# Window attention feeding a two-layer network: output copies ahead of a global softmax, early scores for a step's second head, and keys split two heads ahead

## The chip, the cores and the metric

The kernel runs on one core of one Trainium2 chip. Its time is the device time of one execution in microseconds (us), and the time of a kernel is the median over several runs. The engines are named as the profile names them: PE (TensorE matmul) with PEld (its weight load), DVE (VectorE), ACT (ScalarE), POOL (GpSimd), and SP, whose queue (SPq) issues the DMA transfers.

## What is computed

Eight sequences have eight heads each, with 512 local and 32 global positions and a head dimension of 64. The reference, cut to what matters:

```python
k_all = np.concatenate([k_g, k_l], axis=2)
v_all = np.concatenate([v_g, v_l], axis=2)
out_g = np.matmul(sm(scale * np.matmul(q_g, k_all.transpose(0, 1, 3, 2))), v_all)
s_ll = scale * np.matmul(q_l, k_l.transpose(0, 1, 3, 2))
mask = np.abs(pos[:, None] - pos[None, :]) <= 32
s_ll = np.where(mask, s_ll, -1000000000.0)
s_lg = scale * np.matmul(q_l, k_g.transpose(0, 1, 3, 2))
out_l = np.matmul(sm(np.concatenate([s_lg, s_ll], axis=-1)), v_all)
x = np.concatenate([out_g, out_l], axis=2)   # rows are tokens after a transpose
r = np.maximum(x @ w_in, 0.0)
out = (s * (r * r) + b) @ w_out
```

The local positions attend to a window and to the global positions. The global positions attend to everything. The 4608 tokens then pass through a network with 512 inputs, 2048 hidden values and 512 outputs.

## The kernel before

A "head" j in the code is one head of one half of a sequence (256 local tokens), so there are 128 of them. A token tile is 256 tokens, the 512 inputs of which are the outputs of eight heads. There are 16 such tiles and a 17th for the global tokens.

The kernel has two parts. The first 16 heads and the first eight steps of the network are written out by hand in a table (`PLAN`). Neither is touched by the change. The second part is a loop over `m`, called step m here, from 8 to 136. Step m does the attention work of one head, or of two in steps 12 and 14 (`TWO_HEADS`), then the first layer for two chunks of hidden values (`ffn_in(m)`), the activation (`relu`, `square`, `g_high`, `g_low`), and the second layer of the step before (`ffn_out(m - 1)`). Step 8 has head 16, step 12 heads 20 and 21, step 14 heads 23 and 24, and from step 15 on step m has head m + 10. A step's first head is `a`, its second is `z` (in the new code).

The work of one head j is:

- `split(j)`: ACT casts keys and queries to a short form (`kq`, two casts, L235 and L237), and POOL subtracts to get the rest (two subtractions, L236 and L238). It needs the loaded `rk` and `rq`.
- `products(j)`: PE computes the local scores into `ps_s` and the global ones into `ps_g`. Each has one buffer, so head j + 1 waits until both were read.
- `sm_scores` (DVE, L250, mask and row minimum, frees `ps_s`), `g_copy` (ACT, `tg`, L430) and `g_add` (DVE, L436, frees `ps_g`), `sm_exp` (ACT, L261), `sm_sums` and `sm_divide` (DVE, L268 to L277).
- `planes(j)`: DVE splits the result into 16-bit planes (`two`, one buffer, L453), and `turn(j)` sends them through a transposing DMA on SP's queue (`turned`, L459). `join(j)` on ACT puts them together one head later (`ptp`, two buffers for two pairs of heads, L467).
- `pv` on PE for four heads at a time (`ps_op`), whose result ACT copies into `x` (L392). For the global rows of half a sequence's heads there are `g_softmax` (DVE maximum L475, ACT exponential L481, DVE division L485 to L487), transposes, `g_pv` on PE, a copy `og` on ACT (L529), and a DMA to `xg_d` (L531).

After the last step of a token tile, `ffn_out` also copies the two accumulators out on ACT (`o`, L633). These tiles share the two buffers of tag `r` with the activations. This happens in the border steps 8, 16, 24 and so on.

On PE, ACT and DVE the order of the instructions is the order in which the code is written (`fixed.enter_context(tc.manual_schedule(...))`). The order on POOL and SP in the loop is made by a scheduler. Every queue is worked off in its order.

Of the kernel before, what the change touches and what calls it, by code (L numbers as in the profile page):

```python
# [11 lines left out]
F32 = mybir.dt.float32  # L12
# [4 lines left out]
I16 = mybir.dt.int16  # L17
# [3 lines left out]
B, H, SL, SG, D = 8, 8, 512, 32, 64  # L21
DM, DF = 512, 2048
P = 128
# [16 lines left out]
SGW = SL + SG  # L40
# [5 lines left out]
NF = 16  # L46
# [21 lines left out]
Q2 Fo6 Fr7 YA0 YA1 YB0 YB1 Fs7 Fb7 Fl7 Q3  # L68
""".split()
G_AT = (12, 16)  # L70
G_TR = 3
G_LD = 2
G_PV = 5


def f32(ap):
# [4 lines left out]
def window_attention_then_ffn(ctx: ExitStack, tc: tile.TileContext, qd, qp, qg, kw, vw, vg, w_in, w_out, out):  # L81
    nc = tc.nc
# [158 lines left out]
    def sm_scores(heads, scores):  # L241
        hf = slot(heads[0])[1]
        nm = sb.tile([P, 4], F32, tag="nm", name=f"nm{heads[0]}")
        parts = []
        for j, p_s in zip(heads, scores):
            sm = st_["p", j] = sb.tile([P, NC], F32, tag="sm", name=f"sm{j}", bufs=4)
            for blk in range(2):
                n, c = len(parts), COLS[hf, blk]
                mask = masks[hf == 0 and blk == 0][:, 0:c.stop - c.start]
                nc.vector.tensor_tensor_reduce(  # L250
                    out=sm[:, c], in0=p_s[:, c], in1=mask,
                    op0=ALU.add, op1=ALU.min, scale=-scale, scalar=BIG, accum_out=nm[:, n:n + 1],
                )
                parts.append(sm[:, c])
        st_["parts", heads[0]] = parts, nm
# [171 lines left out]
    def g_copy(j):  # L427
        ng = 256 + 32 * slot(j)[1]
        tg = st_["tg", j] = sb.tile([P, 288], F32, tag="tg", name=f"tg{j}", bufs=1)
        nc.scalar.copy(out=tg[0:32, 0:ng], in_=st_["pg1", j][32:64, 0:ng])  # L430
# [4 lines left out]
        p_g, tg = st_.pop(("pg1", j)), st_.pop(("tg", j))  # L435
        nc.vector.tensor_add(out=sg_rows(j, 32)[:, hf * 256:hf * 256 + ng], in0=p_g[0:32, 0:ng], in1=tg[0:32, 0:ng])  # L436

    def scores(j):
        products(j)
        sm_scores([j], [st_.pop(("ps1", j))])  # L440
        g_copy(j)
        g_add(j)
        sm_exp(j)
        sm_sums(j)
        sm_divide(j, False)
        planes(j)
# [42 lines left out]
    def g_softmax(b, g):  # L489
        g_max(b, g)  # L490
        g_exp(b, g)
        g_divide(b, g)
# [18 lines left out]
    def g_transposes(b, g):  # L511
        for part in range(2):
            g_turn(b, g, part)
            g_part(b, g, part)
            yield

    def g_load(b, g):
        rv = st_["rvg", b, g] = sb.tile([P, 4, 5, D], F32, tag="vsg", name=f"rvg{b}_{g}", bufs=1)
        nc.sync.dma_start(rv.rearrange("p h c d -> p (h c d)"), vg[b, g])
# [162 lines left out]
    assert not chunk_parts  # L682

    NM = NT * 8
    early, gpv, turns = defaultdict(list), defaultdict(list), {}
    for b in range(B):
        for g in range(2):
            s0 = 16 * b + G_AT[g]
            early[s0].append(lambda b=b, g=g: g_softmax(b, g))
            turns[s0 + G_TR] = g_transposes(b, g)  # L690
            early[s0 + G_LD].append(lambda b=b, g=g: g_load(b, g))
            gpv[s0 + G_PV].append(lambda b=b, g=g: g_pv(b, g))

    def head_work(j):
        if j < NS and j % 4 == 2:
            for i in (j // 2 - 1, j // 2):
                v_load(i)
        if j < NS:
            b1 = j // 16 + 1
            if j % 16 == 14 and b1 < B:  # L700
                qg_load(b1)
            scores(j)
            if j % 16 == 15 and j + 1 < NS:
                qg_split(b1)

    def values(j):
        if NF <= j - 5 < NS and j % 4 == 1:
            pv((j - 5) // 2, 2)
            pv_out((j - 5) // 2)
        for fn in gpv.pop(j, []):  # L710
            fn()

    def join_before(j):
        if NF <= j - 1 < NS:
            join(j - 1)

    def ends(j):
        for fn in early.pop(j, []):
            fn()

    load(NF + 2)
    j = NF
    for m in range(8, NM + 1):
        heads = [j, j + 1] if m in TWO_HEADS else [j]
        j = heads[-1] + 1
        a = heads[0]
        if a + 1 < NS:
            split(a + 1)
        for i in heads:
            if i + 3 < NS:  # L730
                load(i + 3)
        head_work(a)
        for i in heads[1:]:
            split(i + 1)
        values(a)
        t = m // 8 + 1
        if m < NM:
            ffn_in(m)
            if m % 8 == 7 and t < 16:
                x_split(t)  # L740
            relu(m)
            join_before(a)
            for c in LATER.get(m, ()):
                chunk_high(c)
            square(m)
            for c in LATER.get(m, ()):
# [7 lines left out]
        ends(a)  # L754
        for i in heads[1:]:
            head_work(i)
            values(i)
            join_before(i)
            ends(i)
        turn_g = [turns.pop(i) for i in heads if i in turns]  # L760
        ffn_out(m - 1, turn_g[0] if turn_g else iter(()))
    assert all(k < NF for d in (early, gpv, turns) for k in d)
    fixed.close()


# [74 lines left out]
```

## Time and profile before

| | |
|---|---|
| median of 3 runs | 968.01 us (967.84 to 969.32) |
| the profiled execution's own time | 969.22 us |
| its span, first to last instruction | 967.4 us |
| busy in the span | PE 937.0, PEld 837.2, DVE 649.1, ACT 708.7, POOL 219.0 us |

Most of the table speaks of the span of one profiled execution. Some 1.8 us of the execution's time lie around the span. A share of busy time is a mean over all stages, and the stages of this kernel have different limits.

### The profile page before, as it was taken

The numbers are of one execution on the slowest core, as the hardware profiler recorded it, in microseconds if no ns is written. First come the engines' busy times: TensorE is split into PE (matmuls) and PEld (weight loads), VectorE is DVE, ScalarE is ACT, GpSimd is POOL, SyncE is SP. The second block draws the span as 40 slices with busy tenths as digits, with TensorE's granted clock in tenths as the row PEclk, the third lists the DMA queues.
The fourth block names the chain that finished last, engine by engine and source line by source line (L and its number), as shares of the span: only waits on it lengthen the run. The fifth ranks groups of instructions, "written<-read, shape, count | busy, mean of one in ns | idle before, by whom it ended". The sixth has DMA issues, their size and how long they took to land.

```text
span 967.4 us, 20021 instructions
## 1 busy us (share of the span) xinstructions
PE 937.0 (97%) x7328; PEld 837.2 (87%) x7328; DVE 649.1 (67%) x1988; ACT 708.7 (73%) x1514; POOL 219.0 (23%) x245
## 2 busy tenths in 40 slices
PE   7899898999999999999999999999999999999996
PEld 3658787999999999999999999999999999988995
DVE  6999877777667666676667766776667766742221
ACT  6899687788778877788778877887788877742321
POOL 1010232232232322223323232332323222200000
PEclk7999999999999999999999999999999999999999
DMA  9953454454544564454454554456544554321000
GB/s 332 368 183 102 111 134 106 117 119 122 129 106 111 140 133 97 113 132 124 108 117 105 139 133 103 113 126 147 103 106 97 135 134 111 71 53 34 22 1 22
DMA packets 177610, 115.09 MB, mean 119 GB/s; under 512 B 125800, under 2 KB 166760, under 8 KB 177512
## 3 DMA queue, kind: packets, MB, share of 16 engines
q1 hardware_dynamic: 177368, 113.60, 45.1%
q8 instruction: 58, 0.95, 0.4%
q14 instruction: 40, 0.33, 0.1%
q10 hardware_dynamic: 144, 0.21, 0.1%
HBM read 74.98 MB, written 9.44 MB: 87 GB/s over the span
## 4 chain that ended last, share of the span: by engine, by line
PE 83%; DVE 9%; DMA 3%; ACT 2%; issue 1%; SPq 0%; DVEq 0%; ACTq 0%
PE ps_h L586 36%; PE acc L625 34%; PE ps_op L380 5%; PE ps_s L418 4%; DMA wst<-in_w_out 2%; DVE wst L184 2%; DVE we L190 1%; PE ps_g L422 1%; DVE wl L207 1%; PE ps_og L527 1%; DMA turned<-two 1%; PE ps_tg L505 1%; DVE we L174 1%; DVE r L598 1%; DVE g L606 1%
## 5 line engine op out<-in xcount | busy, mean ns | idle before, releaser
L586 PE MATMUL ps_h<-xs,wh 128*128 128x256 f32 x1584 | 288.2, 282 | 3.5 <-DVE r L598 2.8
L236 POOL TENSOR_TENSOR kq<-rk,kq 64x416 fp32r<-64x416 f32 x112 | 127.9, 1142 | 595.9 <-ACT kq L235 569.9
L625 PE MATMUL acc<-wh,g 128*128 128x512 f32 x792 | 248.9, 395 | 1.6 <-ACT o L633 1.6
L586 PEld LDWEIGHTS ps_h<-xs,wh 128*128 128x128 f32 x1584 | 243.4, 189 | 6.8 <-DVE r L598 3.0
L586 PE MATMUL ps_h<-xs,wl 128*128 128x256 f32 x792 | 220.1, 281 | 0.8 <-DVE wl L207 0.8
L606 DVE SCALAR_TENSOR_TENSOR g<-r,sb_t,g 128x512 fp32r<-128x512 f32 x133 | 100.5, 755 | 108.5 <-ACT g L602 108.5
L625 PEld LDWEIGHTS acc<-wh,g 128*128 128x128 f32 x792 | 140.6, 188 | 26.8 <-ACT o L633 1.8
L594 ACT ACTIVATE r<-ps_h 128x512 f32<-128x512 f32 x136 | 81.2, 597 | 107.7 <-PE ps_h L586 102.1
L625 PE MATMUL acc<-wl,g 128*128 128x512 f32 x396 | 155.2, 392 | 0.0
L467 ACT COPY ptp<-turned 128x1024 int16<-128x1024 int16 x112 | 152.0, 1358 | 1.5 <-DMA turned<-two 1.5
L586 PEld LDWEIGHTS ps_h<-xs,wl 128*128 128x128 f32 x792 | 149.4, 189 | 1.0 <-DVE wl L207 1.0
L598 DVE SCALAR_TENSOR_TENSOR r<-ps_h,sb_t,r 128x512 f32<-128x512 f32 x136 | 101.7, 748 | 67.3 <-ACT r L594 65.5
L602 ACT ACTIVATE g<-r,sb_t 128x512 fp32r<-128x512 f32 (+1 forms) x136 | 98.2, 722 | 57.2 <-DVE r L598 57.1
L261 ACT ACTIVATE sm<-sm,nm 128x224 f32<-128x224 f32 (+1 forms) x256 | 117.5, 460 | 6.4 <-DVE nm L250 3.7
L586 PE MATMUL ps_h<-xs,w 128*128 128x256 f32 x816 | 103.3, 282 | 0.0
L453 DVE COPY two<-sm 128x256 int16<-128x256 int16 x448 | 101.3, 291 | 1.9 <-DMA turned<-two 1.8
L586 PEld LDWEIGHTS ps_h<-xs,w 128*128 128x128 f32 x816 | 98.7, 189 | 2.0 <-issue 0.2
L625 PE MATMUL acc<-w,g 128*128 128x512 f32 x408 | 99.4, 392 | 0.1
L625 PEld LDWEIGHTS acc<-wl,g 128*128 128x128 f32 x396 | 74.3, 188 | 16.8
L625 PEld LDWEIGHTS acc<-w,g 128*128 128x128 f32 x408 | 74.2, 188 | 14.9 <-DVE g L606 0.5
L238 POOL TENSOR_TENSOR kq<-rq,kq 128x256 fp32r<-128x256 f32 x112 | 83.6, 747 | 8.8
L418 PE MATMUL ps_s<-kq 128*128 128x192 f32 (+1 forms) x448 | 78.6, 265 | 3.1 <-DVE nm L250 2.3
(77 smaller groups left out, 1123.6 us busy)
## 6 DMA issues: line engine op xcount, KB each, us to landing
rvp<-in_vw SPq DMA_DIRECT2D x64, 256.0 KB, 3.3
rq<-in_qd SPq DMA_DIRECT2D x112, 128.0 KB, 2.2
rk<-in_kw SPq DMA_DIRECT2D x56, 208.0 KB, 2.4
rvg<-in_vg SPq DMA_DIRECT2D x16, 640.0 KB, 4.7
out<-o SPq DMA_DIRECT2D x34, 256.0 KB, 2.1
wst<-in_w_in SPq DMA_DIRECT2D x16, 512.0 KB, 6.1
wst<-in_w_out SPq DMA_DIRECT2D x16, 512.0 KB, 6.9
turned<-two SPq DMA_TRANSPOSE x112, 3.1
```

Source lines behind the costliest of these rows:

```text
L236: nc.gpsimd.tensor_sub(out=ks[p1:p1 + 64], in0=rk[p0:p0 + 64], in1=f32(ks[p0:p0 + 64]))
L238: nc.gpsimd.tensor_sub(out=qs[:, 1, :], in0=rq, in1=f32(qs[:, 0, :]))
L261: nc.scalar.activation(out=p, in_=p, func=AF.Exp, bias=nm[:, n:n + 1], scale=-1.0, accum_out=ss[:, n:n + 1],)
L418: nc.tensor.matmul(p_s[:, cols], lhsT=qs[:, a, blk * P:(blk + 1) * P], rhs=ks[:, cols], start=(a == 0), stop=(a == 1),)
L453: nc.vector.tensor_copy(out=two[:, 2 * blk + c], in_=sm[:, :, c0:c0 + P])
L467: nc.scalar.copy(out=pt.bitcast(I16).rearrange("p c (q h) -> p c h q", h=2), in_=st_.pop(("turned", j)))
L586: nc.tensor.matmul(p_h[:, k], lhsT=weight(f, a)[:, c * P:(c + 1) * P], rhs=xcur[t][:, c, :] if m < PLAIN else xs_[t][:, e, c, :], start=(n ...
L594: nc.scalar.activation(out=r, in_=st_["ph", m], func=AF.Relu)
L598: nc.vector.scalar_tensor_tensor(out=r, in0=st_.pop(("ph", m)), scalar=s_t, in1=r, op0=ALU.mult, op1=ALU.mult)
L602: nc.scalar.activation(out=as_used(m, g[:, int(m < PLAIN)]), in_=st_["r", m], func=AF.Identity, bias=b_t)
L606: nc.vector.scalar_tensor_tensor(out=g[:, 1], in0=st_.pop(("r", m)), scalar=b_t, in1=f32(g[:, 0]), op0=ALU.add, op1=ALU.subtract,)
L625: nc.tensor.matmul(oacc[t][i], lhsT=as_used(m, g[:, a, k, i * P:(i + 1) * P]), rhs=weight(f, e)[:, 512:1024], start=(pr == 0 and n == 0), ...
```

## The change

The loop is written anew. Work per head and per step is the same, and no instruction is added or taken away. Four things move.

1. `split` runs two heads ahead in place of one. Step 10 (`CATCH_UP`) has one more split to get there. From then on step m splits head a + 2.
2. In a step with two heads, the products and the score maximum of the second head (`begin(z)`) come right after `ffn_in(m)`, ahead of the planes and the transposing DMA of the first (`turned(a)`). The rest of the second head (`weigh(z)`) stays behind `g_low(m)`.
3. In such a step `pv`, its copy, `g_pv` and its copy (`values(z)`) come behind `ffn_out(m - 1)`. They stood ahead of it and ahead of `join`.
4. The global softmax of the second half of the heads of sequence 0 moves from step 8 to step 9, and in border steps what is listed as `early` comes behind `ffn_out` with its output copies.

The functions `g_planes`, `g_turn_dma` and `g_join` are new, but with `G_PE = 8` and eight sequences no step calls them.

```diff
-            early[s0].append(lambda b=b, g=g: g_softmax(b, g))
+            early[s0 + int((b, g) == (0, 1))].append(lambda b=b, g=g: g_softmax(b, g))
...
+        if cut < NS and cut <= a + 2:
+            split(cut)
+            cut += 1
+        if a < NS:
+            begin(a)
+            weigh(a)
+        if z > a:
+            split(cut)
+            cut += 1
+        elif m == CATCH_UP:
+            split(cut)
+            cut += 1
+        if z == a:
+            values(a)
+        if m < NM:
+            ffn_in(m)
+            if z > a:
+                begin(z)
+        if a < NS:
+            turned(a)
...
+        if not border:
+            at(early, a)
+        if z > a:
+            weigh(z)
+            turned(z)
+            join_before(z)
...
         ffn_out(m - 1, turn_g[0] if turn_g else iter(()))
+        if border:
+            at(early, a)
+        if z > a:
+            values(z)
```

On ACT, from the end of step 8 to step 10, this stood before (`sg4` is the global score tile of the moved softmax, `o0_0` and `o0_1` are the output copies):

```order
L602 ACTIVATE g8_1137<-r8_1130,sb_t_71 128x512
L481 ACTIVATE sg4_226,gs0_1_1143<-sg4_226,gm0_1_1140 128x544
L633 COPY o0_0_1160<-acc0_0_557 128x512
L633 COPY o0_1_1163<-acc0_1_558 128x512
L235 CAST kq18_1166<-rk18_1065 64x416
...
L602 ACTIVATE g9_1261<-r9_1252,sb_t_71 128x512
L235 CAST kq19_1278<-rk18_1065 64x416
```

Now the same stretch of ACT reads as follows, up to the activation of step 10:

```order
L659 COPY o0_0_1152<-acc0_0_557 128x512
L659 COPY o0_1_1155<-acc0_1_558 128x512
L235 CAST kq18_1162<-rk18_1065 64x416
...
L628 ACTIVATE g9_1253<-r9_1244,sb_t_71 128x512
L485 ACTIVATE sg4_226,gs0_1_1259<-sg4_226,gm0_1_1256 128x544
L235 CAST kq19_1284<-rk18_1065 64x416
...
L261 ACTIVATE sm18_1297,ss18_1303<-sm18_1297,nm18_1296 128x224
L235 CAST kq20_1310<-rk20_1158 64x416
L237 CAST kq20_1310<-rq20_1160 128x256
L620 ACTIVATE r10_1347<-ps_h10_1315 128x512
```

The softmax went behind the activation of step 9, and step 10 got the casts of a second head.

On ACT in step 12, from the global copy of head 21 on, this stood before:

```order
L430 COPY tg21_1543<-ps_g21_1533 32x256
L261 ACTIVATE sm21_1540,ss21_1546<-sm21_1540,nm21_1539 128x192
L261 ACTIVATE sm21_1540,ss21_1546<-sm21_1540,nm21_1539 128x224
L392 COPY x2_1577<-ps_op8_1560 128x512
L529 COPY og0_1_1600<-ps_og0_1_1579 128x64
L467 COPY ptp10_1603<-turned20_1493 128x4x2x128
L235 CAST kq23_1617<-rk22_1368 64x416
```

Now the two copies `x2` and `og0_1` stand behind the join of head 20, which waits for a transposing DMA:

```order
L261 ACTIVATE sm21_1531,ss21_1551<-sm21_1531,nm21_1530 128x224
L471 COPY ptp10_1565<-turned20_1539 128x4x2x128
L392 COPY x2_1596<-ps_op8_1579 128x512
L555 COPY og0_1_1619<-ps_og0_1_1598 128x64
L235 CAST kq24_1628<-rk24_1462 64x416
```

On SP's queue of the new kernel the transfers of the same step stand like this. The store to `xg_d` stands ahead of the transposing DMA of head 21, as it did before, but it needs the copy `og0_1`, which is what moved:

```order
L463 DMA_TRANSPOSE turned20_1539<-two20_1534 128x8x128
L314 DMA rvp10_1624<-in_vw 128x2x256
L314 DMA rvp11_1626<-in_vw 128x2x256
L545 DMA rvg1_0_2362<-in_vg 128x1280
L557 DMA xg_d_112<-og0_1_1619 4x32x64
L463 DMA_TRANSPOSE turned21_1563<-two21_1558 128x8x128
```

On DVE in step 12 the new kernel has the score maximum of head 21 between the division and the planes of head 20:

```order
L277 TENSOR_SCALAR sm20_1479<-sm20_1479,ss20_1486 128x224
L250 ISA sm21_1531,nm21_1530<-ps_s21_1523,mask1_87 128x192
L250 ISA nm21_1530 128x1
L250 ISA sm21_1531,nm21_1530<-ps_s21_1523,mask0_95 128x224
L250 ISA nm21_1530 128x1
L457 COPY two20_1534<-sm20_1479 128x256 x4
```

Before, the maximum of head 21 stood behind `g_low(12)` there.

## Rows read from the trace of the kernel before

**Rows 1.** The span and the mean granted clock of the core.

```profile
core 0: 967.4 us, clock 0.989
```

**Rows 2.** Stretch, length, busy PE, PEld, DVE, ACT, POOL (instructions), granted clock, DMA, GB/s.

```profile
105.00:157.00 52.00, 45.34 (x382) 39.69 (x381) 39.89 (x126) 40.80 (x89) 16.13 (x18) 1.00 0.55 132
157.00:900.00 743.00, 743.00 (x6015) 679.04 (x6015) 501.49 (x1667) 564.03 (x1207) 194.61 (x210) 1.00 0.46 112
```

**Rows 3.** Waits of PE, 98 to 165 us: total, times, longest.

```profile
PE ps_s L418 <- DVE nm L250: 2.3, 1, 2.3
PE acc L625 <- ACT o L633: 1.6, 1, 1.6
...
PE ps_op L380 <- ACT ptp L467: 0.6, 1, 0.6
PE ps_s L418 <- POOL kq L238: 0.4, 1, 0.4
```

**Rows 4.** The chain that ended last, from 109 us: start, length, what.

```profile
123.09 4.76 DMA turned<-two
...
136.57 4.58 DMA turned<-two
```

**Rows 5.** Timeline of ACT, then DVE, steps 8 and 9: start, length, instruction, idle before.

```profile
108.20 0.73 ACT L602 ACTIVATE g<-r,sb_t 128x512 fp32r<-128x512 f32 x1 [1.21 <-DVE r L598]
...
112.50 0.54 ACT L235 CAST kq<-rk 64x416 fp32r<-64x416 f32 x1
...
109.21 0.75 DVE L606 SCALAR_TENSOR_TENSOR g<-r,sb_t,g 128x512 fp32r<-128x512 f32 x1
...
112.08 0.50 DVE L487 TENSOR_SCALAR sg<-sg,gs 128x544 f32<-128x544 f32 x1
```

**Rows 6.** Timeline of DVE, then POOL, heads 19 and 20 (steps 11 and 12).

```profile
127.29 0.57 DVE L277 TENSOR_SCALAR sm<-sm,ss 128x192 f32<-128x192 f32 x2
127.95 0.90 DVE L453 COPY two<-sm 128x256 int16<-128x256 int16 x4
...
133.77 1.43 DVE L277 TENSOR_SCALAR sm<-sm,ss 128x192 f32<-128x192 f32 x2
135.12 1.42 DVE L453 COPY two<-sm 128x256 int16<-128x256 int16 x4
...
133.77 1.07 POOL L236 TENSOR_TENSOR kq<-rk,kq 64x416 fp32r<-64x416 f32 x1 [0.26 <-ACT kq L235]
134.92 0.86 POOL L238 TENSOR_TENSOR kq<-rq,kq 128x256 fp32r<-128x256 f32 x1
```

**Rows 7.** Timeline of ACT, then SP's queue, end of step 12.

```profile
140.09 0.58 ACT L392 COPY x<-ps_op 128x512 f32<-128x512 f32 x1
140.58 0.22 ACT L529 COPY og<-ps_og 128x64 f32<-128x64 f32 x1
141.17 1.37 ACT L467 COPY ptp<-turned 128x1024 int16<-128x1024 int16 x1 [0.37 <-DMA turned<-two]
...
140.82 0.56 SPq L531 DMA_DIRECT2D xg_d<-og  x1
...
142.17 1.24 SPq L459 DMA_TRANSPOSE turned<-two  x1
```

**Rows 8.** The transposing DMA (tile `turned`), 100 to 200 us.

```profile
DMA to landing us min/median/max: 3.0/3.1/4.8
```

**Rows 9.** Timeline of DVE, then PE, steps 14 and 15.

```profile
155.30 0.75 DVE L606 SCALAR_TENSOR_TENSOR g<-r,sb_t,g 128x512 fp32r<-128x512 f32 x1 [0.79 <-ACT g L602]
...
156.55 0.44 DVE L436 TENSOR_TENSOR sg<-ps_g,tg 32x288 f32<-32x288 f32 x1
...
157.17 0.30 PE L422 MATMUL ps_g<-kq,qgs 128*64 128x288 f32 x1
```

**Rows 10.** Busy time and granted clock in two short stretches, columns as in rows 2.

```profile
154.00:157.00 3.00, 0.71 (x5) 0.32 (x4) 2.20 (x7) 1.72 (x5) 0.00 (x0) 1.00 0.63 136
157.00:162.00 5.00, 5.00 (x47) 4.60 (x47) 3.94 (x17) 4.16 (x11) 1.79 (x2) 0.66 0.50 83
```

More of the change, by code (lines that the diff above doesn't have):

```diff
@@ L70 @@
 G_AT = (12, 16)
-G_TR = 3
-G_LD = 2
 G_PV = 5
+G_PE = 8
+CATCH_UP = 10
 def f32(ap):
@@ L436, in g_add, with begin, weigh @@
         nc.vector.tensor_add(out=sg_rows(j, 32)[:, hf * 256:hf * 256 + ng], in0=p_g[0:32, 0:ng], in1=tg[0:32, 0:ng])
-    def scores(j):
+    def begin(j):
         products(j)
         sm_scores([j], [st_.pop(("ps1", j))])
+    def weigh(j):
         g_copy(j)
@@ L445, in scores, with turned @@
         sm_divide(j, False)
+    def turned(j):
         planes(j)
@@ L515, in g_transposes, with g_planes, g_turn_dma, g_join @@
             yield
+    def g_planes(b, g, c0, c1):
+        if c0 == 0:
+            two = sb.tile([P, 20 * P], I16, tag="vsg", name=f"gtwo{b}_{g}", bufs=1)[:, 0:10 * P]
+            st_["gtwo", b, g] = two.rearrange("p (c h k) -> p c h k", c=5, h=2)
+        sg = st_["sg", b, g].bitcast(I16).rearrange("p (k h) -> p h k", h=2)
+        for c in range(c0, c1):
+            s0 = min(c * P, SGW - P)
+            nc.vector.tensor_copy(out=st_["gtwo", b, g][:, c], in_=sg[:, :, s0:s0 + P])
+    def g_turn_dma(b, g):
+        both = sb.tile([P, 2 * JOINED[0][1]], I16, tag="pg", name=f"pg{b}_{g}", bufs=1)
+        turned, pg = both[:, 0:10 * P].rearrange("p (c h q) -> p c h q", c=5, h=2), both[:, 10 * P:20 * P]
+        nc.sync.dma_start_transpose(
+            turned.rearrange("p c h q -> p (c h) q"), st_.pop(("gtwo", b, g)).rearrange("p c h k -> p (c h k)"),
+        )
+        st_["turned_g", b, g] = turned, pg
+    def g_join(b, g, c0, c1):
+        turned, pg = st_["turned_g", b, g]
+        nc.scalar.copy(out=pg.rearrange("p (c q h) -> p c h q", c=5, h=2)[:, c0:c1], in_=turned[:, c0:c1])
+        st_["pg", b, g] = pg.bitcast(F32).rearrange("p (c r) -> p c r", c=5)
     def g_load(b, g):
@@ L684, in window_attention_then_ffn @@
     NM = NT * 8
-    early, gpv, turns = defaultdict(list), defaultdict(list), {}
+    early, gpv, joins_at, planes_at, turns = defaultdict(list), defaultdict(list), defaultdict(list), defaultdict(list), {}
     for b in range(B):
@@ L688, in window_attention_then_ffn, with head_loads @@
             s0 = 16 * b + G_AT[g]
-            early[s0].append(lambda b=b, g=g: g_softmax(b, g))
-            turns[s0 + G_TR] = g_transposes(b, g)
-            early[s0 + G_LD].append(lambda b=b, g=g: g_load(b, g))
+            early[s0 + int((b, g) == (0, 1))].append(lambda b=b, g=g: g_softmax(b, g))
+            if b < G_PE:
+                turns[s0 + 3] = g_transposes(b, g)
+                early[s0 + 2].append(lambda b=b, g=g: g_load(b, g))
+            else:
+                planes_at[s0 + 1].append(lambda b=b, g=g: g_planes(b, g, 0, 3))
+                planes_at[s0 + 2].append(lambda b=b, g=g: (g_planes(b, g, 3, 5), g_turn_dma(b, g)))
+                joins_at[s0 + 3].append(lambda b=b, g=g: (g_join(b, g, 0, 2), g_load(b, g)))
+                joins_at[s0 + 4].append(lambda b=b, g=g: g_join(b, g, 2, 5))
             gpv[s0 + G_PV].append(lambda b=b, g=g: g_pv(b, g))
-    def head_work(j):
+    def head_loads(j):
         if j < NS and j % 4 == 2:
@@ L697, in head_work, with at @@
                 v_load(i)
[L698 to L704, printed above, removed]
+        if j < NS and j % 16 == 14 and j + 16 < NS + 2:
+            qg_load(j // 16 + 1)
+    def at(hooks, j):
+        for fn in hooks.pop(j, []):
+            fn()
     def values(j):
@@ L709, in values @@
             pv_out((j - 5) // 2)
-        for fn in gpv.pop(j, []):
-            fn()
+        at(gpv, j)
     def join_before(j):
@@ L715, in join_before @@
             join(j - 1)
-    def ends(j):
-        for fn in early.pop(j, []):
-            fn()
     load(NF + 2)
-    j = NF
+    j, cut = NF, NF + 1
     for m in range(8, NM + 1):
@@ L725, in window_attention_then_ffn @@
         j = heads[-1] + 1
-        a = heads[0]
-        if a + 1 < NS:
-            split(a + 1)
+        a, z = heads[0], heads[-1]
+        border = (m - 1) % 8 == 7
         for i in heads:
@@ L731, in window_attention_then_ffn @@
                 load(i + 3)
[L732 to L735, printed above, removed]
+        for i in heads:
+            head_loads(i)
+        if cut < NS and cut <= a + 2:
[18 more added lines that the diff above has]
+            turned(a)
+            if a % 16 == 15 and a + 1 < NS:
+                qg_split(a // 16 + 1)
         t = m // 8 + 1
         if m < NM:
-            ffn_in(m)
             if m % 8 == 7 and t < 16:
@@ L742, in window_attention_then_ffn @@
             join_before(a)
+            at(joins_at, a)
             for c in LATER.get(m, ()):
@@ L745, in window_attention_then_ffn @@
             square(m)
+            at(planes_at, a)
             for c in LATER.get(m, ()):
@@ L753, in window_attention_then_ffn @@
             join_before(a)
[L754 to L759, printed above, removed]
+            at(joins_at, a)
+            at(planes_at, a)
+        if not border:
[4 more added lines that the diff above has]
+            join_before(z)
+            at(joins_at, z)
+            at(planes_at, z)
+            at(early, z)
         turn_g = [turns.pop(i) for i in heads if i in turns]
         ffn_out(m - 1, turn_g[0] if turn_g else iter(()))
-    assert all(k < NF for d in (early, gpv, turns) for k in d)
+        if border:
+            at(early, a)
+        if z > a:
+            values(z)
+    assert all(k < NF for d in (early, gpv, turns, joins_at, planes_at) for k in d)
     fixed.close()
```

## The prediction

> **What bounds the kernel now.** I read the span first [rows 1], then busy time by stretch, then what PE waits for, then the chain that ended last, and last the timelines of the engines in the stretch where PE waits. The reader is to see that there are two regimes. From 157 to 900 us PE is busy for 743.00 of 743.00 us at a granted clock of 1.00 [rows 2]: no order of other work can give anything there, and another order takes something only if it makes an engine late by more than its slack, and DVE and ACT are busy for only 501 and 564 us of it. From 105 to 157 us PE is busy for 45.34 of 52 us [rows 2], so 6.7 us is all that PE idles in the steps 8 to 15 that the change rearranges. PE's waits name the objects: 2.3 us for the score maximum, 1.6 us for the output copies, 0.6 us for a join, 0.4 us for a split [rows 3]; the rest are waits of under 1 us. The chain that ended last shows what makes PE wait there: before 157 us it runs mostly over ACT, DVE and two transposing DMAs of 4.76 and 4.58 us [rows 4], not over PE. In these steps the limit is a relay of ACT, DVE and the transposes, in which PE waits now at one place and now at another. So the question is what the change does to the relay, and the end of the kernel moves by what PE's restart near 157 us moves by.
>
> **Splits two ahead.** From step 15 on, a split has a step's time or more in hand, and PE's only wait for one that I count is 0.4 us, in step 14 [rows 3]. So in the steady steps this is worth nothing. Its price is the extra split in step 10. Its casts lie under ACT's wait for DVE, but its two POOL subtractions now fall beside head 18's division and planes, as they do in step 12 for head 20 already. What that does is in the trace: for head 19, with POOL quiet, division and planes take 0.57 and 0.90 us, for head 20, beside POOL subtractions of 1.07 and 0.86 us, they take 1.43 and 1.42 us [rows 6]. This is 0.86 + 0.52 = 1.4 us on DVE, and `square(10)`, which all that follows hangs on, stands behind them. In steps 12 and 14 the slow place exists before and after. The bounds are 0 (the subtractions fall a little earlier or later) and 1.4 us. I take **+1.2**, near the upper end, since the step has the same form.
>
> The Trainium skill (SBUF — State Buffer, Who interferes with whom) has a rule that speaks against this change: VectorE's copies and tensor_scalar operations in their two-port mode and GpSimd's operations exclude each other from a shared pair of ports, and the loser stands still for the other's whole instruction. By that rule the price would be up to both subtractions, 1.07 + 0.86 = 1.9 us, and the whole sum below 0.7 us higher; the row's 1.4 us is less, so I keep the row.
>
> **The softmax one step later.** Before, ACT ends `g_high(8)` at 108.93, waits for DVE's maximum, does the exponential and the two output copies, and only at 112.50 comes to the next cast; DVE's `g_low(8)` starts at 109.21 and ends at 109.96 [rows 5]. Now the first copy can start near 109.0. The second takes the buffer that `g_low(8)` reads, so it starts at 109.96 and ends about 0.5 us later, half the 0.96 us that both take in the chain; the cast comes at about 110.5, 2.0 us earlier, and PE's 1.6 us wait for the copies is gone. But the softmax now stands whole between `g_low(9)` and the score maximum of head 18. In step 8 DVE has from 109.96 to 112.58 for it, the end of its division (112.08 + 0.50) [rows 5], 2.6 us, which now delays head 18 because DVE's maximum and ACT's exponentials of head 18 queue behind it. The net is 2.6 - 2.0 = **+0.6**. The bounds are -2.0 (all of the second is hidden) and +1.0. This is a stall that moves: PE has it next at `ffn_out(10)`, waiting for `g_low(10)`.
>
> **The second head's early scores, step 12.** The score maximum of head 21 goes ahead of the planes of head 20. Its length is what lies between `g_low` and `g_add` in step 14, from 156.05 to 156.55 [rows 9], 0.5 us. Planes 20, `turn(20)` and `square(12)` come that much later; but the planes then fall behind POOL's subtractions in place of beside them, which gives back up to 0.5 us (1.42 - 0.90) [rows 6]. I take **+0.2**, between 0 and 0.5.
>
> **The late values, step 12.** Before, the copies `x` and `og` (0.58 and 0.22 us) lie in ACT's wait for the transposing DMA, ahead of the join at 141.17, and the `xg_d` store goes out at 140.82 in time for the transposing DMA of head 21 at 142.17 [rows 7]. Now they come behind the join. From the landing of transpose 20, ACT has the join (1.2 us of its 1.37, since the next one overlaps), and 0.5 + 0.2 us of copies, and the store takes 0.56 us on SP: 2.5 us until `turn(21)` can be issued, where it was 1.0 us (141.17 to 142.17). This is +1.5 us on SP's queue, and +0.7 us on ACT's next cast and copy, which DVE's `g_add(22)` waits for. Behind the store are queued the transposes 21 and all later loads, and DVE's planes 22 wait for transpose 21 because `two` has one buffer. Some of it was slack: transpose 21 landed near 145.3 (142.17 and the median 3.1) [rows 7, 8]. I take **+1.1**. The bounds: +1.5, and if transpose 20, which took 4.6 us [rows 4], now lands after the 3.1 us median [rows 8] because the `rvp` loads moved behind it, 1.5 us less, that is -0.4.
>
> **Step 14.** The score maximum of head 24 again goes ahead of planes 23 (+0.2, as above), but `g_add(24)` then follows `g_low(14)` directly, without the 0.5 us between them and a little of waiting [rows 9], -0.6. So **-0.4**. PE no longer waits 2.3 us for `ps_s`. It waits for `ps_g`, which `g_add(24)` frees: the products of head 25 get through their first three matmuls and stop there.
>
> **The sum** is 1.2 + 0.6 + 0.2 + 1.1 - 0.4 = +2.7 us. PE's `ps_g` matmul moves from 157.17 [rows 9] to about 159.9, and from there PE is the limit as before. The profiled execution took 969.22 us, so this form would take 971.9; against the median of 968.01, which is 1.2 us lower, it is **970.7 us**, 0.28% more.
>
> **The clock.** Right after PE's 2.3 us idle before 157 us, in a stretch where it was busy for 0.71 of 3.00 us, the granted clock falls, and is 0.66 on average from 157 to 162 us [rows 10]: the lower of the two levels for about two thirds of it, which costs (1 - 0.66) x 5.0 = 1.7 us of PE's work. The shorter waits left the clock at 1.00 [rows 2]. In the new form PE's idle time ahead of `ps_g` is about as long, so I take the drop as kept, 0 us. If it vanished it would give 1.7 us, and a further one would take as much where PE is not waiting anyway.
>
> **The rivals.** *PE's waits are the loss themselves (faster).* If the relay had room, each removed wait would count: 1.6 + 2.3 + 0.6 + 0.4 = 4.9 us, and with the clock drop gone another 1.7, so 968.0 - 4.9 = 963.1, at the least 961.4. For it speaks that each of these waits is at a point that the change touches; against it that the chain runs over the others there. It decides if DVE is through with `g_add(24)` before 155.0, that is if the terms sum to less than -1.9 us. A part of it, one of the costs absent and the clock drop gone, gives 964 to 966. Chance 0.15. *The costs mostly miss (no difference).* Transpose 20 lands after 3.1 us (-1.5) and the extra subtractions fall half beside idle DVE (-0.6): 970.7 - 2.1 = 968.6. The rows give both ends of both, so chance 0.33. *The change does nothing in the steady steps* is part of all cases: there it only makes a split earlier that nobody waits for.
>
> **How the numbers follow.** My forecast, slower by over 0.2% (about what a measurement of this kernel can tell from no change, 1.9 us), has a chance of 0.52. With the rival of no difference at 0.33 and the faster one at 0.15, these are also the chances of the three verdicts. The lower end of the range takes the sum without POOL's term (-1.2), with the fast transpose (-1.5) and without the clock drop (-1.7): 966.3. The upper end takes the upper bounds (1.4, 1.0, 0.5, 1.5 and 0, in all 4.4): 972.4, rounded to 972.6 for a drop that comes partly on top. What lies below 966.3 is some 0.12, above 972.6 some 0.06. The forecast's own range is 969.9 to 972.6.
>
> **What would show it right or wrong.** The wait of PE for the output copies in step 9 is gone, and a new one of 1 us or more stands at `ffn_out(10)` or at the next products. Division or planes of head 18 take over 1 us each beside POOL. ACT's `x` and `og` copies come right behind a join that waited, and SP's transposing DMA of head 21 follows the `xg_d` store at once. The last wait of PE near 159 us is for `ps_g`, on `g_add`, of 2 us or more, with a clock drop behind it, and after that the busy share of PE is full. I am wrong in the relay if `g_add(24)` ends before 156 us, in the POOL term if head 18 shows 0.57 and 0.90 us, in the late values if transpose 21 is issued less than 1.5 us after transpose 20 landed, and in the frame if PE waits after 165 us.

## The result, and the profile after

The changed kernel takes **973.95 us** (median of 6 runs, 973.65 to 976.11) against 968.02 us (967.84 to 969.50) for the kernel before in the same comparison: ratio 1.0062, interval 1.0052 to 1.0072, that is +5.9 us where +2.7 us was forecast, and outside the range given. The profiled execution took 973.65 us, against 969.22 us. This is +4.4 us; the rest is that the profiled execution of before lay 1.2 us above its median and this one 0.3 us below.

The same views in the same order. The span and mean clock, as [rows 1], then windows of both regimes (columns as in [rows 2]), with the stretch in which the clock now falls last:

```profile
core 0: 971.9 us, clock 0.989
```

```profile
105.00:162.00 57.00, 47.42 (x385) 41.33 (x383) 40.01 (x128) 41.46 (x92) 18.13 (x20) 0.97 0.51 121
162.00:904.00 742.00, 741.15 (x6008) 677.30 (x6009) 502.62 (x1669) 563.35 (x1207) 192.47 (x208) 1.00 0.46 112
119.00:126.00 7.00, 6.08 (x24) 5.25 (x25) 5.38 (x15) 4.75 (x14) 2.33 (x3) 0.76 0.05 12
```

From 162 us on PE is busy for 741.15 of 742.00 us, nearly as full as before from 157 us. So the loss lies ahead of that, in the relay of steps 8 to 15. PE idles there for 9.6 of 57 us, where it was 6.7 of 52 us [rows 2]. What it waits for, from 100 to 175 us (total, times, longest), answers to [rows 3]:

```profile
PE ps_g L422 <- DVE sg L436: 3.8, 3, 2.7
PE ps_h L612 <- ACT wh L202: 3.4, 1, 3.4
PE ps_s L418 <- DVE nm L250: 1.8, 1, 1.8
PE ps_h L612 <- DVE wl L207: 0.8, 1, 0.8
PE ps_op L380 <- ACT ptp L471: 0.4, 1, 0.4
```

The 1.6 us for the output copies are gone, and a wait of 3.4 us for ACT's cast of the weights is new. That cast is not late by itself. ACT's timeline of steps 8 and 9 (start, length, instruction, idle before it and who ended it) shows what stands ahead of it, beside [rows 5]:

```profile
108.65 0.72 ACT L628 ACTIVATE g<-r,sb_t 128x512 fp32r<-128x512 f32 x1 [1.20 <-DVE r L624]
109.28 0.56 ACT L659 COPY o<-acc 128x512 f32<-128x512 f32 x1
110.50 0.59 ACT L659 COPY o<-acc 128x512 f32<-128x512 f32 x1 [0.66 <-DVE g L632]
110.98 0.54 ACT L235 CAST kq<-rk 64x416 fp32r<-64x416 f32 x1
...
116.40 0.60 ACT L620 ACTIVATE r<-ps_h 128x512 f32<-128x512 f32 x1 [3.03 <-DMA out<-o]
...
118.08 1.03 ACT L202 CAST wh<-we 128x1024 fp32r<-128x1024 f32 x1
```

The copies and the cast come where the prediction has them, the cast at 110.98 us. But then `relu(9)` waits **3.03 us for the output store**: its tile `r` gets a buffer that the store still reads, since `o` and `r` share two buffers. SP's queue of the changed kernel and the time from a store's issue to its landing (the view gives one landing for the two stores), then the same in the kernel before, with ACT's `relu(9)` there and the instruction ahead of it:

```profile
107.98 1.97 SPq L463 DMA_TRANSPOSE turned<-two  x1
110.06 0.51 SPq L545 DMA_DIRECT2D rvg<-in_vg  x1
110.63 0.89 SPq L663 DMA_DIRECT2D out<-o  x2
...
DMA to landing us min/median/max: 5.8/5.8/5.8
```

```profile
112.15 0.82 SPq L637 DMA_DIRECT2D out<-o  x2
...
DMA to landing us min/median/max: 2.7/2.7/2.7
...
114.68 0.21 ACT L529 COPY og<-ps_og 128x64 f32<-128x64 f32 x1
114.98 0.60 ACT L594 ACTIVATE r<-ps_h 128x512 f32<-128x512 f32 x1
```

The stores go out 1.5 us earlier than before, and `relu(9)` starts 1.4 us later: at 116.40 us with the landing, where it was 114.98 us, 0.13 us behind a landing at 112.15 + 2.7 = 114.85 us. (The whole profile starts 0.46 us later; counted from `g_low(8)` the stores go out 2.0 us earlier and `relu(9)` starts 1.0 us later.) The store held `relu(9)` in the kernel before, too, for a time too short for the list of waits: there it starts 0.30 us behind the start of `og`, the instruction ahead of it, and 0.11 us behind it in a kernel in which it waits for no store (e2, below). So what moves earlier ahead of `relu(9)` gains nothing behind it as long as the store lands no earlier. The reader can find this only by asking who has the buffer next.

The other places, one fence for each group: head 18 on DVE and POOL (as [rows 6]), the end of step 12 on ACT and SP's queue (as [rows 7]), step 14 on DVE and PE (as [rows 9]).

```profile
125.67 1.36 DVE L277 TENSOR_SCALAR sm<-sm,ss 128x192 f32<-128x192 f32 x2
126.94 1.44 DVE L457 COPY two<-sm 128x256 int16<-128x256 int16 x4
...
125.58 1.08 POOL L236 TENSOR_TENSOR kq<-rk,kq 64x416 fp32r<-64x416 f32 x1 [0.17 <-ACT kq L235]
126.74 0.89 POOL L238 TENSOR_TENSOR kq<-rq,kq 128x256 fp32r<-128x256 f32 x1
```

```profile
144.84 1.37 ACT L471 COPY ptp<-turned 128x1024 int16<-128x1024 int16 x1 [0.52 <-DMA turned<-two]
146.23 0.59 ACT L392 COPY x<-ps_op 128x512 f32<-128x512 f32 x1
146.72 0.22 ACT L555 COPY og<-ps_og 128x64 f32<-128x64 f32 x1
...
141.63 1.23 SPq L463 DMA_TRANSPOSE turned<-two  x1
...
146.96 0.56 SPq L557 DMA_DIRECT2D xg_d<-og  x1
147.61 1.24 SPq L463 DMA_TRANSPOSE turned<-two  x1
```

```profile
161.27 0.75 DVE L632 SCALAR_TENSOR_TENSOR g<-r,sb_t,g 128x512 fp32r<-128x512 f32 x1 [0.79 <-ACT g L628]
161.94 0.44 DVE L436 TENSOR_TENSOR sg<-ps_g,tg 32x288 f32<-32x288 f32 x1
...
162.44 0.35 PE L422 MATMUL ps_g<-kq,qgs 128*64 128x288 f32 x1 [2.73 <-DVE sg L436]
```

### The profile page after: what moved, and what is told of

Its sections match the earlier page's. It is cut to its first block, busy times and chain, and to the rows that moved or that the text cites. A ratio compares the mean times of both kernels' runs of the same rounds, so it can differ in the third digit from the quotient of the medians.

```text
span 971.9 us, 20030 instructions
## 1 busy us (share of the span) xinstructions
PE 936.7 (96%) x7328; PEld 836.9 (86%) x7328; DVE 649.8 (67%) x1988; ACT 708.4 (73%) x1514; POOL 218.4 (22%) x245
## 4 chain that ended last, share of the span: by engine, by line
PE 83%; DVE 9%; DMA 3%; ACT 2%; issue 2%; SPq 0%; DVEq 0%; ACTq 0%
PE ps_h L612 36%; PE acc L651 35%; PE ps_op L380 5%; PE ps_s L418 4%; DVE wst L184 2%; DMA wst<-in_w_out 1%; PE ps_g L422 1%; DVE wl L207 1%; DVE we L190 1%; PE ps_og L553 1%; PE ps_tg L509 1%; DVE r L624 1%; DVE we L174 1%; DMA turned<-two 1%; DVE sm L250 1%
```

## The experiments

Twelve kernels ran, each timed in 5 rounds beside the kernel before. Runs of one kernel spread over 1.7 to 6 us here, so the table gives the ratio to the kernel before with its interval, and that ratio times 968.02 us. The next columns are starts of DVE instructions in the profiled execution, counted from `g_low(8)`, ahead of which nothing differs (109.21 us before, 109.67 us after, 108.2 to 110.4 us in the others). "Wait" is that of `relu(9)` for the store as the view lists it; in e1 `relu(9)` is idle for 0.34 us, which the view puts down to PE, and a wait for the store isn't ruled out there. The last column has the granted clock from 119 to 126 us and from 150 to 170 us. A value of 0.91 in these 20 us is a drop that takes some 1.7 us of PE's work.

| kernel | ratio | us | wait | g_add 18 | g_low 10 | g_low 12 | g_low 13 | g_add 24 | clock |
|---|---|---|---|---|---|---|---|---|---|
| before | 1 | 968.0 | 0 | 11.08 | 15.31 | 28.78 | 39.00 | 47.34 | 1.00, 0.91 |
| after | 1.0062 [1.0052, 1.0072] | 974.0 | 3.03 | 14.60 | 20.16 | 33.38 | 44.49 | 52.27 | 0.76, 1.00 |
| e1 border back | 1.0025 [1.0015, 1.0035] | 970.4 | 0 | 11.32 | 16.84 | 30.13 | 42.00 | 49.77 | 1.00, 0.91 |
| e2 `o` elsewhere | 1.0016 [1.0007, 1.0026] | 969.6 | 0 | 10.77 | 16.34 | 29.58 | 41.46 | 49.23 | 1.00, 0.91 |
| e3 one ahead | 1.0044 [1.0032, 1.0056] | 972.3 | 2.92 | 14.49 | 18.71 | 32.07 | 43.45 | 51.22 | 0.61, 0.91 |
| e4 values back | 1.0064 [1.0051, 1.0076] | 974.2 | 3.21 | 14.79 | 20.34 | 33.61 | 44.38 | 52.16 | 0.53, 0.91 |
| e5 load late | 1.0054 [1.0041, 1.0067] | 973.2 | 0 | 11.51 | 17.08 | 31.33 | 42.30 | 50.08 | 1.00, 0.91 |
| e6 before + border | 1.0048 [1.0035, 1.0061] | 972.7 | 3.03 | 14.60 | 18.81 | 32.11 | 42.48 | 50.82 | 0.53, 0.91 |
| e7 before + border + `o` | 0.9994 [0.9985, 1.0003] | 967.4 | 0 | 10.77 | 14.99 | 28.27 | 38.03 | 46.38 | 1.00, 1.00 |
| e8 mended | 0.9998 [0.9988, 1.0007] | 967.8 | 0 | 10.76 | 14.99 | 28.33 | 38.73 | 46.51 | 1.00, 1.00 |
| e9 early scores in 14 alone | 0.9990 [0.9979, 1.0001] | 967.1 | 0 | 10.76 | 14.99 | 28.26 | 38.57 | 46.38 | 1.00, 0.91 |
| e10 mended + extra split | 1.0012 [1.0001, 1.0023] | 969.2 | 0 | 10.77 | 16.34 | 29.53 | 40.50 | 48.29 | 1.00, 0.91 |
| e11 the same, written later | 1.0022 [1.0013, 1.0031] | 970.2 | 0 | 10.76 | 16.32 | 29.58 | 40.24 | 48.02 | 1.00, 0.91 |
| e12 e9 + extra split | 1.0019 [1.0009, 1.0029] | 969.9 | 0 | 10.76 | 16.32 | 29.44 | 39.99 | 47.77 | 1.00, 0.91 |

**The border part (e1).** In the changed kernel:

```
-            early[s0 + int((b, g) == (0, 1))].append(lambda b=b, g=g: g_softmax(b, g))
+            early[s0].append(lambda b=b, g=g: g_softmax(b, g))
...
-        if not border:
-            at(early, a)
+        at(early, a)
...
-        if border:
-            at(early, a)
```

> The changed kernel with the border part alone undone: the softmax of the second group of heads stands at the end of step 8, ahead of the output copies, as before. Its time is 973.95 us with the border part. Theory 'store' (the output store lands late, at 116.4 us, and relu of step 9 waits 3.0 us for a buffer that it still reads): the wait goes, head 18's score maximum starts 3 to 3.5 us earlier than 123.56 us, and the time is 970.5 to 971.0 us, or up to 1.7 us more if the clock falls behind PE's last wait near 160 us. Theory 'softmax' (the softmax ahead of head 18's maximum is the price, as the prediction has it, with 0.6 us net): 973.3 us. Theory 'elsewhere' (the loss stems from the splits and the step with two heads): 973.9 us, unchanged.

`g_add(18)` comes 3.3 us earlier, the time falls by (1.0062 - 1.0025) x 968 = 3.6 us. The loss is mostly in this part, and "elsewhere" falls; it doesn't yet tell the store from the softmax.

**The output tiles in another buffer (e2).**

```
+            if t == 0:
+                o_pg = sb.tile([P, JOINED[0][1]], F32, tag="pg", name="o0", bufs=1)
             for i in range(2):
-                o = sb.tile([P, DM], F32, tag="r", name=f"o{t}_{i}", bufs=2)
+                if t == 0:
+                    o = o_pg[:, i * DM:i * DM + DM]
+                else:
+                    o = sb.tile([P, DM], F32, tag="r", name=f"o{t}_{i}", bufs=2)
```

> The changed kernel, with the two output tiles of the first token group in the buffer of the transposed global scores (free at that time) in place of the two buffers that relu's result r uses in turn. Nothing else moves. Theory 'store': relu of step 9 starts near 113.4 us in place of 116.40, since no buffer of it is read by a store any more; the time is 971 us, or up to 1.7 us more if the clock drop comes back behind PE's last wait near 160 us. Theory 'softmax': relu starts earlier, but DVE's softmax and division keep head 18's maximum where it is, near 123 us, and the time is 973.5 us or more.

ACT's `relu(9)` with the instruction ahead of it, and the landing of a store in this kernel:

```profile
111.62 0.21 ACT L555 COPY og<-ps_og 128x64 f32<-128x64 f32 x1
111.73 0.60 ACT L620 ACTIVATE r<-ps_h 128x512 f32<-128x512 f32 x1
...
DMA to landing us min/median/max: 5.9/5.9/5.9
```

The stores still take 5.9 us, but nobody waits for them. `g_add(18)` comes 14.60 - 10.77 = **3.83 us** earlier, and the time falls by 4.5 us, somewhat more than "store" said. The softmax stays where the change put it, so the prediction's softmax theory falls. Its net effect alone is 10.77 - 11.08 = -0.3 us, not +0.6.

**What holds the stores up (e5).** The load that stands ahead of them goes out elsewhere:

```
-        nc.sync.dma_start(rv.rearrange("p h c d -> p (h c d)"), vg[b, g])
+        queue = nc.scalar if (b, g) == (0, 1) else nc.sync
+        queue.dma_start(rv.rearrange("p h c d -> p (h c d)"), vg[b, g])
```

> The changed kernel with the 640 KB load of the second group's global values (rvg, first token group) moved from SP's queue, where it goes out 0.6 us ahead of the output store, to ACT's queue at its place in the program, the end of step 10. The buffers are as in the changed kernel, so relu of step 9 still needs the store to have landed. Theory 'load ahead' (the store lands 5.8 us after its issue because its data goes behind this load's): it lands 2.7 us after its issue or sooner, relu waits under 0.5 us in place of 3.0, and the time is that of the kernel with the output tiles elsewhere, 1.0016 of the kernel before, or up to 0.3 us more for the issue on ACT. Rival 'the transpose ahead' (what holds the store is the transposing DMA of head 16, which stands ahead of both): the store still takes over 4.5 us, relu waits 2 us or more, and the ratio stays near 1.006.

SP's queue and ACT's `relu(9)`, then DVE's planes of head 19 in this kernel:

```profile
109.30 1.57 SPq L664 DMA_DIRECT2D out<-o  x2
...
112.69 0.61 ACT L621 ACTIVATE r<-ps_h 128x512 f32<-128x512 f32 x1
...
130.46 0.90 DVE L457 COPY two<-sm 128x256 int16<-128x256 int16 x4 [0.92 <-DMA turned<-two]
```

`relu` waits for no store, so the store that it would wait for, the first of the two, landed by 112.69 us, at most 3.4 us after its issue: the 640 KB load ahead of it was what held it, and "the transpose ahead" falls. The time was forecast wrongly, though: only 0.8 us of the 4.3 us come back. Some of that is seen. The load in its new place goes beside the transposing DMA of head 18, planes 19 wait 0.92 us for that DMA, and the clock falls behind 157 us, where it didn't in the changed kernel. From `g_add(18)` to `g_add(24)` this kernel takes 38.6 us, the changed kernel 37.7 us. At `g_add(24)` it is still 2.2 us ahead of the changed kernel, and the clock, 0.87 over the 13 us from 157 to 170 us, takes up to (1 - 0.87) x 13 = 1.7 us of that. This leaves 0.5 us, near the 0.8 us of the medians.

**The border part alone (e6, e7).** In the kernel before, first alone, then with the output tiles as in e2:

```
-            early[s0].append(lambda b=b, g=g: g_softmax(b, g))
+            early[s0 + int((b, g) == (0, 1))].append(lambda b=b, g=g: g_softmax(b, g))
...
-        ends(a)
+        border = (m - 1) % 8 == 7
+        if not border:
+            ends(a)
...
+        if border:
+            ends(a)
```

> The kernel before with the border part alone: output copies ahead of the softmax, which stands one step later. Theory 'store': relu of step 9 waits 3 us for the store, head 18's score maximum is 3.5 us later than in the kernel before, and the ratio to it is 1.0030 to 1.0040. Theory 'softmax' as in the prediction: 0.6 us, ratio 1.0006. If the loss needs the other parts as well (keys split ahead, step with two heads), the ratio is below 1.0015 too, but with relu's wait in the trace.

> The kernel before with the border part and with the first token group's output tiles in the buffer of the transposed global scores, so that relu of step 9 waits for no store. What is left is the softmax one step later. From the trace of the changed kernel with the output tiles elsewhere: head 18's score maximum starts 10.1 us after g_low of step 8, where it is 10.38 us in the kernel before; ratio 0.9997, that is no difference. The prediction's term of 0.6 us says 11.0 us and 1.0006. Its lower bound, all of the second softmax stall hidden, says 8.4 us and 0.998.

Waits of ACT in e6, from 100 to 175 us, with the landing of the stores, and the same landing in e7:

```profile
ACT r L594 <- DMA out<-o: 3.0, 1, 3.0
...
DMA to landing us min/median/max: 5.6/5.6/5.6
```

```profile
DMA to landing us min/median/max: 5.6/5.6/5.6
```

The wait needs none of the other three parts. With it the border part costs 0.0048 x 968 = 4.6 us, more than expected; without it the ratio is 0.9994 and its interval includes 1, as "-0.3 us" said. In e7 the lower bound of the prediction (8.4 us for head 18's score maximum) is missed as well: it starts at 10.07 us, where it was 10.38 us.

**The extra split (e3, e10, e11).** e3 takes the three lines of `CATCH_UP` out of the changed kernel. e10 puts them into the mended kernel (e8, below), and e11 has them behind `turned(a)`:

```
-        elif m == CATCH_UP:
-            split(cut)
-            cut += 1
```

> The changed kernel without the extra split of step 10, so that keys are split one head ahead throughout. Theory 'POOL beside DVE': division and planes of head 18 fall from 1.36 and 1.44 us to 0.57 and 0.90 us, and the time falls by 1.2 to 1.3 us to 972.7 us. Rival: DVE's loss there is hidden behind the wait that follows, or the split that then stands in step 12 brings PE's wait for the keys back; time 973.5 to 974.2 us.

> The mended kernel with the extra split of step 10 put back, at its place in the changed kernel. Theory 'POOL beside DVE': division and planes of head 18 take 1.36 and 1.44 us in place of 0.57 and 0.89, g_low of step 10 comes 1.3 us later, ratio 0.9998 + 0.0014 = 1.0011. Rival 'earlier keys pay': PE's waits for POOL's subtractions, 1.6 us in all in the mended kernel, go, and the ratio is 0.9998 or below.

> As the kernel with the extra split put back, but the split stands behind the planes of head 18, so that POOL's subtractions fall beside square, low weights and g_low of step 10 in place of division and planes. Theory 'POOL stops copies and scalings' (only the two-byte copies and the scaling of plain SBUF tiles suffer): division and planes take 0.57 and 0.89 us, the others their usual 0.75 us, and the ratio is that of the mended kernel, 0.9998, or less by PE's waits for keys. Rival 'POOL slows whatever DVE does': one of the others grows by 0.5 us or more and the ratio is 1.0005 to 1.0011. Third: ACT's two casts now stand ahead of relu of step 10 and delay it by 0.95 us: 1.0008.

DVE and POOL at head 18 in e3, for comparison with the fence above:

```profile
125.44 0.56 DVE L276 TENSOR_SCALAR sm<-sm,ss 128x192 f32<-128x192 f32 x2
125.92 0.89 DVE L456 COPY two<-sm 128x256 int16<-128x256 int16 x4
...
123.20 1.17 POOL L235 TENSOR_TENSOR kq<-rk,kq 64x416 fp32r<-64x416 f32 x1 [9.76 <-ACT kq L234]
124.44 0.74 POOL L237 TENSOR_TENSOR kq<-rq,kq 128x256 fp32r<-128x256 f32 x1
```

Without the second pair of subtractions, division and planes take 0.56 and 0.89 us. Taken apart, the loss lies in two instructions. The first division and the first copy of the planes, in the changed kernel (with the second division between them), then in e3:

```profile
125.67 1.11 DVE L277 TENSOR_SCALAR sm<-sm,ss 128x192 f32<-128x192 f32 x1
126.70 0.32 DVE L277 TENSOR_SCALAR sm<-sm,ss 128x224 f32<-128x224 f32 x1
126.94 0.83 DVE L457 COPY two<-sm 128x256 int16<-128x256 int16 x1
...
125.44 0.32 DVE L276 TENSOR_SCALAR sm<-sm,ss 128x192 f32<-128x192 f32 x1
...
125.92 0.29 DVE L456 COPY two<-sm 128x256 int16<-128x256 int16 x1
```

Each of the two begins while a POOL subtraction runs and ends 0.12 and 0.14 us behind that subtraction's end (126.66 and 127.63 us); the others keep their time. The two lose 0.79 + 0.54 = 1.33 us. From `g_add(18)` to `g_low(10)` it is 5.56 us in the changed kernel and 4.22 us in e3, and 5.57 us in e10 against 4.23 us in e8: **1.34 us** each time. The times follow, by 1.7 us (e3) and 1.4 us (e10). e11 told nothing of its question, since `turned(a)` has no work on ACT or POOL and every engine got its instructions in the same order as in e10. So e10 and e11 are one schedule timed twice, 1.0012 and 1.0022: differences of 0.001 between two kernels aren't to be read here.

**The late values (e4).**

```
             turned(z)
+            values(z)
             join_before(z)
...
-        if z > a:
-            values(z)
```

> The changed kernel with the second head's values products and copies back where they were, ahead of the join of head 20 (in step 14 of head 23). Theory 'late values' as predicted: the copies and the store of xg_d then lie in ACT's wait for the transposing DMA, its successor is issued right behind its landing, and the time falls by 1.1 us to 972.9 us. Rival, from the traces of both kernels: what the late values cost is given back by the transposing DMA of head 20, which took 3.2 us in place of 4.6 us with the loads behind it; with the values back it takes 4.6 us again, and the time is 973.5 to 974.3 us.

No difference: +0.2 us by the ratios. In its profile the transposing DMA of head 20 was issued at 141.56 us and landed near 146.5 us, 5.0 us, where the changed kernel took 3.2 us. That gives the rival right by its words. But see the last section: that DMA took between 3.1 and 5.0 us in kernels with the same order of SP's queue around it. A second pair, e2 (values late) against e10 (values back), shows no difference either: 1.0016 and 1.0012.

**The mended versions (e8, e9, e12).** e8 joins the edits of e2, e3 and e4. e9 is e8 with `begin(z)` behind `g_low` in step 12, and e12 is e9 with the extra split as in e11.

```
-            if z > a:
+            if z > a and m == 14:
                 begin(z)
...
         if z > a:
+            if m == 12:
+                begin(z)
             weigh(z)
```

> The changed kernel with three things mended: the first token group's output tiles in the buffer of the transposed global scores, no extra split in step 10, the second head's values products and copies back where they were. What is left is the border part without its wait and the second head's early scores. By the steps of the traces: -0.3 us for the border, 0 for POOL, +0.5 us between g_low 12 and 13, -0.6 us in step 14: -0.4 us, ratio 0.9995, no difference. If PE's waits that are gone count after all: 1.6 us and a clock drop of 1.7 us less, ratio 0.997. If the early scores cost more without the extra split (PE waited 2.6 us for POOL's subtraction in the variant without it): 1.001 to 1.002.

> The mended kernel (output tiles elsewhere, one split ahead, values back) with the second head's early scores in step 14 alone; in step 12 the products and the score maximum of head 21 stand behind the feed-forward part again. From the traces: the early scores cost 0.7 us in step 12 (g_low 13 comes 10.4 us after g_low 12, 9.8 us without them) and give 1.1 us in step 14 (g_low 15 comes 11.2 us after g_low 14, 12.4 us without them). Theory 'two signs': g_low 15 comes 62.0 us after g_low 8 where it is 62.7 us with both and 63.86 us in the kernel before; ratio 0.9985 to 0.9993. Theory of the prediction (+0.2 and -0.4 us): 62.5 us. If PE's longer wait ahead of the later step brings a clock drop: 1.000 to 1.001.

> The kernel with the extra split behind the planes and the early scores in step 14 alone, the version that the steps so far point to. If both terms add up as in the two kernels they come from: 0.9985 to 0.9993, g_low 15 at 62.0 us after g_low 8. If the extra split costs wherever it stands: 0.9998 to 1.0005.

All of the 5.9 us is back in e8 (0.9998) and e9 (0.9990), but none of e7, e8 and e9 is shown to be faster than the kernel before, since their intervals all include 1. "Two signs" wasn't borne out in step 12: `g_low(13)` comes 10.31 us after `g_low(12)` in e9 and 10.40 us in e8, so the early scores don't cost the 0.7 us there that I had read from e7 and e8. (e7 and e9 have the same order on ACT and DVE up to there, but 9.76 and 10.31 us.) e12 falls short of its first expectation and goes past the second (1.0019): the extra split costs there too.

## Why the prediction was wrong

What held: the direction, the frame (no wait of PE behind 165 us, the loss in the relay), and most of the sum's terms. `g_add(24)` comes 52.27 - 47.34 = 4.93 us later relative to `g_low(8)`. Between the marks of the table this is +3.52 to `g_add(18)`, +1.33 to `g_low(10)`, -0.25 to `g_low(12)`, +0.89 to `g_low(13)` and -0.56 to `g_add(24)`. In the times, one part added after the other, the ratios go 0.9994 (e7, the border part without the store's wait), 0.9998 (e8, early scores), 1.0012 (e10, extra split), 1.0016 (e2, late values) and 1.0062 (the changed kernel, with the wait): steps of -0.6, +0.4, +1.4, +0.4 and +4.5 us. Of these only the last is far above what two timings of one schedule differ by (1.0 us, e10 and e11).

- **Splits two ahead**: predicted +1.2, measured +1.34 in two pairs of kernels (after and e3, e10 and e8) and +1.33 in two others (after and before, e12 and e9), from the prediction's row. The rule of the Trainium skill that the prediction weighed (SBUF — State Buffer, Who interferes with whom) lets the one that comes second stand still for the other's whole instruction, and the trace agrees with it: the two DVE instructions that began while POOL was busy ended behind POOL's. What was too high is the 1.9 us that the prediction drew from the rule, because each of the two would have taken some 0.3 us of that time in any case.
- **The softmax one step later**: predicted +0.6 between -2.0 and +1.0, measured +3.52. **This is the step that failed**, and in it the gain of 2.0 us. The other item, 2.6 us for the softmax between `g_low(9)` and head 18, came as forecast: from `g_low(9)` to `g_add(18)` it is 3.98 us where it was 1.36 us (`g_low(9)` and `g_add(18)` after and before, in the fences below). The cast, too, came 2.0 us earlier, counted from `g_low(8)`. But the gain ended at `relu(9)`: `g_low(9)` starts 10.62 us after `g_low(8)`, where it was 9.72 us, so +0.90 in place of -2.0, and 0.90 + 2.62 = 3.52. What the prediction left out is that the copies' tiles are read by a store, and that `relu(9)` takes the buffer of one of them next. It took the earlier copies for a gain, but with the load right ahead of them in SP's queue the stores landed no earlier for going out earlier. e2, e6 and e7 show that it is the wait for the store (without it `g_low(9)` starts at 6.79 us in e2, and `g_add(18)` 3.83 us earlier than in the changed kernel), and e5 that the load is the reason. The buffers' sharing stood in the description of the kernel, and was not priced.

```profile
120.29 0.74 DVE L632 SCALAR_TENSOR_TENSOR g<-r,sb_t,g 128x512 fp32r<-128x512 f32 x1
...
124.27 0.42 DVE L436 TENSOR_TENSOR sg<-ps_g,tg 32x256 f32<-32x256 f32 x1
```

```profile
118.93 0.74 DVE L606 SCALAR_TENSOR_TENSOR g<-r,sb_t,g 128x512 fp32r<-128x512 f32 x1
...
120.29 0.42 DVE L436 TENSOR_TENSOR sg<-ps_g,tg 32x256 f32<-32x256 f32 x1
```

- **Early scores, step 12**: predicted +0.2. From `g_low(11)` to `g_low(12)` it is 7.59 us where it was 7.69 us: nothing to be seen.
- **The late values**: predicted +1.1 between -0.4 and +1.5, measured +0.89 in the changed kernel. It went as described, with the copies right behind a join that waited 0.52 us and the transposing DMA right behind the store (147.61 us, 2.8 us after the landing of the one before). In e1 and e2 the same stretch takes 11.9 us, +1.66; there that DMA landed 4.9 to 5.0 us after its issue. But e4 against the changed kernel, and e10 against e2, show that undoing it gives no time back, so as a cause of the time it is not shown.
- **Step 14**: predicted -0.4, measured -0.56, with the wait for `ps_g` (2.73 us) in place of that for `ps_s` there, as forecast (the 1.8 us for `ps_s` in the list of waits end earlier, at 155.64 us).
- **The clock**: predicted as kept behind the last wait. There it isn't: PE waits 2.73 us before 162.44 us, and the clock stays at 1.00 from 157 to 170 us. So of the 5.27 us by which PE's `ps_g` matmul is later, `ffn_out(14)` is only 4.43 us later (168.16 against 163.73 us). The clock falls in the changed kernel behind the new wait, to 0.76 from 119 to 126 us, 0.53 to 0.61 in the other kernels that have the wait (e3, e4, e6), and not at all (1.00) in the kernels that haven't. From 100 to 180 us the mean clock is 0.98 before and after, so the changed kernel has its drop earlier rather than none. In e1 and e2 it fell earlier too, from 151 to 158 us, behind waits of 2.55 and 2.54 us for `ps_s`.

The faster rival is out for its own reason: PE's wait for the output copies went away, and e7 shows that its 1.6 us, with the softmax moved and nothing new in the way, are worth 0.3 us at head 18 and nothing that the times can tell.

## What to carry to other kernels

When an instruction whose result is stored moves earlier, follow the tile to its end: which queue the store is in, what transfer stands ahead of it there, and who gets the buffer next. A store issued earlier landed no sooner here with a large load right ahead of it, and a buffer that came free 0.13 us ahead of its next use was a wait already. When several parts are changed at once, count the terms from a mark ahead of them all (here `g_low(8)`), because starts and clock drops shift whole profiles by more than a term.

## What was not expected of the hardware

**The stores land behind the load.** Issued 0.56 to 0.82 us behind a 640 KB load, two stores of 256 KB each landed 5.4 to 6.0 us after their issue in eleven kernels, whether anyone waited for them or not. Issued 2.56 us behind it they took 2.7 us (before) and 2.41 us behind it 3.1 us (e1), and with no such load ahead the first took at most 3.4 us (e5). The Trainium skill (DMA: Bandwidth & Descriptors, Queues, rings and completion order) says that each DMA engine consumes the descriptors of a ring in their order; the rows agree with it in so far as the stores landed behind the load (e3: 116.1 and 115.4 us). The load itself landed 5.5 to 5.7 us after its issue where the stores followed it at once (e3, e6 to e9), and 4.6 us before. No run here shows what makes that difference.

**One transposing DMA, two durations.** Read from its issue to the start of the join that waited for it, that of head 20 took 4.6 us before, 3.2 us after, 4.9 us in e1, 5.0 us in e2 and e4, 3.1 us in e3 and 3.5 us in e5. The changed kernel, e1 and e2 issue the same transfers around it at the same distances (loads 1.3, 2.0 and 2.5 us behind it). What decides is open, and no kernel tried it. It is one candidate for the spread of the runs.

**The clock fell behind some waits of PE and not behind others.** After the wait near 119 us (3.39 and 0.76 us in the changed kernel) it fell in all four kernels that have it. After the last wait for `ps_g`, between 156 and 163 us, it stayed at 1.00 in the changed kernel (2.73 us) and in e8 (1.70 us), and fell in e5, e10, e11 and e12 (2.73 us each) and in e9 (1.71 us). What decides is open.
